# Four attention layers as one stream of units, with norms, projections and output stages woven between them

## The chip, the cores and the metric

One core of a Trainium2 chip. The time is the device time of one execution in microseconds (us); medians are over several executions. The granted TensorE clock is given as a share of full speed.

## The reference

The input is 2048 tokens of 640 features in bf16. Two kinds of layer alternate, A, B, A, B: A attends causally within a window of 256 tokens, B attends to all tokens. Each has 32 heads of 20 features.

```python
x = x + A(layernorm(x), A_wqkv, A_wo)
x = x + B(layernorm(x), B_wqkv, B_wo)
x = x + A(layernorm(x), A_wqkv, A_wo)      # the same weights again
x = x + B(layernorm(x), B_wqkv, B_wo)

def layer(x, wqkv, wo):                    # A and B; cut
    q, k, v = split_heads(x @ wqkv)        # 32 heads of 20
    scores = q @ k.T * 20 ** -0.5
    # A only: keep 0 <= query - key < 256, others to -1e9
    return softmax(scores) @ v @ wo
```

B needs the keys and values of all 2048 tokens before any unit of it can end. A needs only the tokens up to its own.

## The kernel before

A *unit* is four heads (group `g` of 8) by 512 queries (chunk `c` of 4): 32 units per layer. The four heads lie in four bands of 32 partitions. A *bank* is the scores of one head, 128 keys by 512 queries, one PSUM bank. A full unit has 64 banks, a windowed one 12. Three banks make a *tile*: TensorE computes its scores, ScalarE (ACT in the profile) takes the exponential of all three at once, VectorE (DVE) multiplies it with a 0/1 mask in the windowed layers, and two tiles later TensorE multiplies it with V into the unit's one output bank `op`. The rows' sums come from a column of ones in V.

The layers run one after another, each as norm, then projections, then attention, and output stages as units end:

```python
psS = tc.tile_pool(name="psS", bufs=2, space=PSUM)   # scores, 2 x 3 banks
psO = tc.tile_pool(name="psO", bufs=1, space=PSUM)   # op, 1 bank
psM = tc.tile_pool(name="psM", bufs=1, space=PSUM)   # everything else, 1 bank
...
for lidx in range(4):
    ...  # norm of all 16 token blocks, transposed into xnT
    ...  # K of all groups, V of all blocks
    for t in range(len(tiles) + PV_LAG):
        ...
        for u in tiles[t]: project_q(u + 1)            # Q of the next unit, once
        sp = psS.tile(...)                             # scores of tile t
        nc.scalar.activation(out=pt, in_=sp, func=Exp, scale=SCALE)
        if windowed: nc.vector.tensor_tensor(out=pt, in0=pt, in1=mask, op=mult)
        ...                                            # V of tile t - 2 into op
        if end: finish_unit(u)
        run_due()
```

When a unit ends, `finish_unit` copies `op` to SBUF on VectorE (`oT`); only then may the next unit write `op`. Its *tail* follows in small steps that go to and fro between TensorE and VectorE: row sums (`zp`), reciprocals split in two bf16 parts (`hl`), a transpose (`rp`), a copy (`rT`), a spread over the partitions (`zb`), the product (`on`). After eight units of a chunk comes the output projection (`yp`), added to `x_sb`.

The softmax here doesn't subtract the row's maximum and nothing guards it: scores larger than these inputs give would overflow.

Of the kernel before, what the change touches and what calls it, by code (L numbers as in the profile page):

```python
# [7 lines left out]
BF16 = mybir.dt.bfloat16  # L8
# [11 lines left out]
G = 8  # L20
# [4 lines left out]
HD = D // 2  # L25
PV_LAG = 2


@with_exitstack
def kernel(  # L30
# [11 lines left out]
    ctx.enter_context(nc.allow_low_precision("bf16 operands of the matmuls"))  # L42

    const = ctx.enter_context(tc.tile_pool(name="const", bufs=1))
    big = ctx.enter_context(tc.tile_pool(name="big", bufs=1))

    xin = A_x.flatten_outer_dims().rearrange("(t p) d -> p t d", p=P)
    xout = out.flatten_outer_dims().rearrange("(t p) d -> p t d", p=P)

    x_sb = big.tile([P, NT, D], BF16, name="x_sb", tag="x_sb")  # L50
    for c in range(NC):
        nc.sync.dma_start(out=x_sb[:, 4 * c : 4 * c + 4, :], in_=xin[:, 4 * c : 4 * c + 4, :])

    wpads = []
    for which in range(2):
        wq = big.tile([P, KD, G, P], BF16, name=f"wq{which}", tag=f"wq{which}")
        wk = big.tile([P, KD, G, P], BF16, name=f"wk{which}", tag=f"wk{which}")
        wpads.append((wq, wk))
    with tc.tile_pool(name="stg", bufs=2) as stg:
        for which, wqkv in ((0, A_wqkv), (1, B_wqkv)):  # L60
            wq, wk = wpads[which]
            st = stg.tile([P, KD, 2 * D], BF16, name="st", tag="st")
            nc.scalar.dma_start(
                out=st[:], in_=wqkv.rearrange("(c p) f -> p c f", p=P)[:, :, 0 : 2 * D]
            )
            for w, off in ((wq, 0), (wk, D)):
                nc.gpsimd.memset(w[:], 0.0)
                for dc in range(KD):
                    dst = w[:, dc, :, :].rearrange("p g (j m) -> p (g j) m", j=4)[:, :, 0:DH]
                    src = st[:, dc, off : off + D].rearrange("p (h e) -> p h e", h=H)  # L70
                    nc.vector.tensor_copy(out=dst, in_=src)  # L71

    wpool = ctx.enter_context(tc.tile_pool(name="wts", bufs=1))
    lnp = ctx.enter_context(tc.tile_pool(name="lnp", bufs=2))
    xnp = ctx.enter_context(tc.tile_pool(name="xnp", bufs=2))
    qp = ctx.enter_context(tc.tile_pool(name="qp", bufs=3))
    ptp = ctx.enter_context(tc.tile_pool(name="ptp", bufs=4))
    otp = ctx.enter_context(tc.tile_pool(name="otp", bufs=2))
    onp = ctx.enter_context(tc.tile_pool(name="onp", bufs=1))
    rzp = ctx.enter_context(tc.tile_pool(name="rzp", bufs=2))  # L80
    psS = ctx.enter_context(tc.tile_pool(name="psS", bufs=2, space=bass.MemoryType.PSUM))
    psO = ctx.enter_context(tc.tile_pool(name="psO", bufs=1, space=bass.MemoryType.PSUM))
    psM = ctx.enter_context(tc.tile_pool(name="psM", bufs=1, space=bass.MemoryType.PSUM))

    xnT = big.tile([P, KD, S], BF16, name="xnT", tag="xnT")
    kT = big.tile([P, G, S], BF16, name="kT", tag="kT")
    v_all = big.tile([P, NT, H, 32], BF16, name="v_all", tag="v_all")
    nc.gpsimd.memset(v_all[:], 0.0)
    nc.gpsimd.memset(v_all[:, :, :, DH : DH + 1], 1.0)

    nhalf = const.tile([P, 4], F32, name="nhalf", tag="nhalf")
    nc.gpsimd.memset(nhalf[:], -0.5)
    ident = const.tile([P, P], BF16, name="ident", tag="ident")
# [5 lines left out]
    sel4 = const.tile([P, 4], BF16, name="sel4", tag="sel4")  # L99
    nc.vector.tensor_copy(  # L100
        out=sel4[:], in_=ident[:].rearrange("p (j m) -> p j m", j=4)[:, :, DH]
    )

    spread4 = const.tile([32, 4, P], BF16, name="spread4", tag="spread4")
    sp32 = const.tile([32, 2, 16], BF16, name="sp32", tag="sp32")
    nc.vector.tensor_copy(
        out=sp32[:], in_=ident[0:32, 0:32].rearrange("p (n r) -> p n r", n=2)
    )
    sp16 = const.tile([32, 16], BF16, name="sp16", tag="sp16")
    nc.vector.tensor_tensor(out=sp16[:], in0=sp32[:, 0, :], in1=sp32[:, 1, :], op=ALU.add)  # L110
    nc.vector.tensor_copy(
        out=spread4[:].rearrange("p q (j m) -> p (q j) m", m=32),
        in_=sp16[:].unsqueeze(2).to_broadcast((32, 16, 32)),
    )

    masks = const.tile([P, 3, C], BF16, name="masks", tag="masks")
    nc.gpsimd.memset(masks[:], 1.0)

    def mask_block(m, b, ge):
        v = masks[:, m, b * P : (b + 1) * P]  # L120
        if ge:
            nc.gpsimd.affine_select(
                out=v, in_=v, compare_op=ALU.is_ge, fill=0.0,
                base=0, pattern=[[1, P]], channel_multiplier=-1,
            )
        else:
            nc.gpsimd.affine_select(
                out=v, in_=v, compare_op=ALU.is_gt, fill=0.0,
                base=0, pattern=[[-1, P]], channel_multiplier=1,
            )  # L130


    for m, b, ge in (
        (0, 0, False), (0, 1, True), (0, 3, False),
        (1, 1, False), (1, 2, True),
        (2, 0, True), (2, 2, False), (2, 3, True),
    ):
        mask_block(m, b, ge)
# [16 lines left out]
    deferred = []  # L155
    clock = [0]

    def later(n, fn):
        deferred.append((clock[0] + n, fn))

    def run_due(everything=False):
        while deferred and (everything or deferred[0][0] <= clock[0]):
            deferred.pop(0)[1]()

    for lidx in range(4):
        which = lidx % 2
        windowed = which == 0
        wqkv, wo = (A_wqkv, A_wo) if windowed else (B_wqkv, B_wo)
        wq, wk = wpads[which]
        wv = wpool.tile([P, KD, D], BF16, name="wv", tag="wv")  # L170
        nc.sync.dma_start(
            out=wv[:], in_=wqkv.rearrange("(c p) f -> p c f", p=P)[:, :, 2 * D : 3 * D]
        )
        wop = wpool.tile([P, G, D], BF16, name="wop", tag="wop")
        nc.gpsimd.memset(wop[:], 0.0)  # L175
        wo_v = wo.rearrange("(g j e) f -> j e g f", g=G, j=4)
        for j in range(4):
            nc.sync.dma_start(out=wop[32 * j : 32 * j + DH, :, :], in_=wo_v[j])

        with tc.manual_schedule():  # L180

            for c in range(NC):
                mv = lnp.tile([P, 4, 2], F32, name="mv", tag="mv")
                for i in range(4):
                    tb = 4 * c + i
                    stats = lnp.tile([P, 2, 6], F32, name="stats", tag="stats")
                    nc.vector.bn_stats(out=stats[:, 0, :], in_=x_sb[:, tb, 0:HD])
                    nc.vector.bn_stats(out=stats[:, 1, :], in_=x_sb[:, tb, HD:D])
                    nc.vector.bn_aggr(out=mv[:, i, :], in_=stats[:])
# [253 lines left out]
```

## Time and profile before

| | before |
|---|---|
| median of 4 runs beside the changed kernel | 3253.48 us (3252.39 to 3254.67) |
| TensorE busy, mean clock in the stages | 77%, 0.60 to 1.00 |
| ScalarE busy | 70% |
| VectorE busy | 26% |
| HBM traffic | 15 MB, 5 GB/s |

The page, the windows by stage and two timelines are shown in the prediction. Two lines of the list of waits are added here. Each line names the instruction that waited, what released it, the sum in us, the number of waits and the longest.

```profile
PE op L396 <- DVE oT L275: 187.6, 114, 2.7
...
PE pq L258 <- DVE rT L300: 103.1, 58, 2.8
```

### The profile page before, as it was taken

Reading aid. Unit: us, or ns where it says so; the run is one execution under the profiler, and the core shown is the slowest. Engines: PE = TensorE matmul, PEld = TensorE weight load, DVE = VectorE, ACT = ScalarE, POOL = GpSimd, SP = SyncE. Lnnn points to the kernel's source line nnn. Section 1 sums busy time; section 2 is a strip of 40 time slices with the busy share of each in tenths; the row PEclk is TensorE's granted clock in tenths of the full one; section 3 lists DMA queues with packets and bytes.
Section 4 is the critical chain, followed back from the end, with each engine's and each line's share of the span. In section 5 each row is a group of like instructions: output and inputs, shape, how many; then the busy total and the mean of one; then the engine's idle time right before and its main releaser. Section 6 shows DMA issues by size and latency. Waiting matters only on the chain.

```text
span 3250.1 us, 36154 instructions
## 1 busy us (share of the span) xinstructions
PE 2509.4 (77%) x15292; PEld 882.9 (27%) x15424; DVE 836.5 (26%) x1800; ACT 2286.0 (70%) x1815; POOL 74.9 (2%) x58
## 2 busy tenths in 40 slices
PE   1866566988888888888886665678888888888887
PEld 1422223422222222222243222243222222222222
DVE  6355556210100111010045555541111001011101
ACT  1334344499799989979934334337997997997996
POOL 5000000000000000000000000000000000000000
PEclk9966666856655565565587665686656556566555
DMA  2000000000000000000000000000000000000000
GB/s 93 11 1 1 1 1 11 11 1 1 1 1 1 1 1 1 1 1 1 1 11 11 1 1 1 1 11 1 1 1 9 1 1 9 1 1 9 1 1 9
DMA packets 11042, 17.38 MB, mean 5 GB/s; under 512 B 384, under 2 KB 9600, under 8 KB 10880
## 3 DMA queue, kind: packets, MB, share of 16 engines
q1 hardware_dynamic: 9568, 11.80, 1.3%
q10 hardware_dynamic: 1312, 3.28, 0.3%
q8 instruction: 120, 1.97, 0.3%
q14 instruction: 42, 0.34, 0.0%
HBM read 12.45 MB, written 2.62 MB: 5 GB/s over the span
## 4 chain that ended last, share of the span: by engine, by line
ACT 40%; PE 29%; issue 16%; DVE 13%; POOL 1%; DMA 0%; ACTq 0%; POOLq 0%; DVEq 0%
ACT pt L367 40%; PE pq L258 8%; DVE pt L382 5%; PE yp L323 5%; PE sp L354 5%; PE pk L224 4%; PE op L396 3%; PE pv L239 3%; DVE x_sb L329 2%; DVE oT L275 2%; DVE on L309 1%; DVE wq L71 1%; POOL wop L175 1%; PE trp L211 1%; POOL rstd L195 0%
## 5 line engine op out<-in xcount | busy, mean ns | idle before, releaser
L367 ACT ACTIVATE pt<-sp 128x1536 bf16<-128x1536 f32 (+2 forms) x1654 | 2183.7, 1504 | 623.0 <-PE sp L354 617.6
L354 PE MATMUL sp<-qt,kT 32*128 32x512 bf16 (+3 forms) x5504 | 938.9, 509 | 245.5 <-ACT pt L367 243.7
L396 PE MATMUL op<-pt,v_all 128*32 128x512 bf16 (+3 forms) x5504 | 948.6, 523 | 189.6 <-DVE oT L275 187.6
L354 PEld LDWEIGHTS <-kT 32*128 32x128 bf16 x5504 | 300.6, 99 | 834.0 <-issue 824.5
L263 DVE CAST qt<-pq 128x512 bf16<-128x512 f32 x128 | 88.6, 692 | 1465.6 <-PE pq L258 1465.6
L396 PEld LDWEIGHTS <-v_all 128*32 128x32 bf16 x5504 | 188.0, 101 | 807.4 <-issue 807.2
L258 PE MATMUL pq<-xnT,wq 128*128 128x512 bf16 x524 | 253.8, 593 | 130.1 <-DVE rT L300 103.1
L382 DVE TENSOR_TENSOR pt<-pt,masks 128x1536 bf16<-128x1536 bf16 (+4 forms) x384 | 240.1, 654 | 153.0 <-ACT pt L367 152.7
L323 PE MATMUL yp<-wop,on 128*128 128x320 bf16 x1024 | 188.7, 335 | 63.4 <-DVE x_sb L329 60.1
L323 PEld LDWEIGHTS <-on 128*128 128x128 bf16 x1024 | 109.0, 108 | 140.5 <-issue 91.5
L224 PE MATMUL pk<-xnT,wk 128*128 128x512 bf16 x624 | 142.9, 388 | 2.3 <-issue 0.9
L258 PEld LDWEIGHTS <-wq 128*128 128x128 bf16 x640 | 76.9, 129 | 245.1 <-issue 237.6
L215 ACT COPY xnT<-trp 128x640 bf16<-128x640 bf16 x64 | 41.4, 694 | 137.9 <-PE trp L211 137.9
L275 DVE CAST oT<-op 128x512 bf16<-128x512 f32 x128 | 88.0, 687 | 176.9 <-PE op L396 176.8
L231 ACT CAST kT<-pk 128x1024 bf16<-128x1024 f32 x32 | 32.4, 1012 | 114.1 <-PE pk L224 114.1
L309 DVE TENSOR_TENSOR on<-oT,zb 128x512 bf16<-128x512 bf16 x128 | 87.5, 684 | 92.8 <-PE zb L305 92.7
L211 PE MATMUL trp<-ident,xn 128*128 128x128 bf16 x320 | 36.2, 280 | 88.5 <-DVE xn L204 85.9
L329 DVE TENSOR_TENSOR x_sb<-x_sb,yp 128x320 bf16<-128x320 bf16 x128 | 62.2, 486 | 159.5 <-PE yp L323 159.4
L239 PE MATMUL pv<-wv,xnT 128*128 128x320 bf16 x640 | 87.6, 299 | 0.0
L224 PEld LDWEIGHTS <-wk 128*128 128x128 bf16 x640 | 64.2, 100 | 80.3 <-issue 8.9
L305 PE MATMUL zb<-rT,spread 32*128 32x128 bf16 x512 | 70.9, 283 | 4.1 <-DVE rT L300 3.9
L239 PEld LDWEIGHTS <-xnT 128*128 128x128 bf16 x640 | 62.6, 98 | 24.9
(42 smaller groups left out, 589.4 us busy)
## 6 DMA issues: line engine op xcount, KB each, us to landing
x_sb<-in_A_x_dram SPq DMA_DIRECT2D x4, 640.0 KB
out_dram<-x_sb SPq DMA_DIRECT2D x4, 640.0 KB
st<-in_A_wqkv_dram ACTq DMA_DIRECT2D x1, 1600.0 KB
st<-in_B_wqkv_dram ACTq DMA_DIRECT2D x1, 1600.0 KB
wv<-in_A_wqkv_dram SPq DMA_DIRECT2D x2, 800.0 KB
wop<-in_A_wo_dram SPq DMA_DIRECT2D x8, 200.0 KB
wv<-in_B_wqkv_dram SPq DMA_DIRECT2D x2, 800.0 KB
wop<-in_B_wo_dram SPq DMA_DIRECT2D x8, 200.0 KB
```

The lines of the kernel that those rows point to most:

```text
L224: nc.tensor.matmul(pk[:, i, :], lhsT=wk[:, dc, g, :], rhs=xnT[:, dc, (c0 + i) * C : (c0 + i + 1) * C], start=(dc == 0), stop=(dc == KD - 1),)
L239: nc.tensor.matmul(pv[:, i, 0:HD], lhsT=xnT[:, dc, tb * P : (tb + 1) * P], rhs=wv[:, dc, i * HD : (i + 1) * HD], start=(dc == 0), stop=(dc ...
L258: nc.tensor.matmul(pq[:], lhsT=wq[:, dc, g, :], rhs=xnT[:, dc, c * C : (c + 1) * C], start=(dc == 0), stop=(dc == KD - 1),)
L263: nc.vector.tensor_copy(out=qt[:], in_=pq[:])
L275: nc.vector.tensor_copy(out=oT[:], in_=ops.pop(u)[:])
L309: nc.vector.tensor_tensor(out=on[:, g, :], in0=oT[:], in1=zb[:], op=ALU.mult)
L323: nc.tensor.matmul(yp[:], lhsT=on[:, g, qb * P : (qb + 1) * P], rhs=wop[:, g, i * HD : (i + 1) * HD], start=(g == 0), stop=(g == G - 1),)
L329: nc.vector.tensor_tensor(out=xv, in0=xv, in1=yp[:], op=ALU.add)
L354: nc.tensor.matmul(sp[:, i, col * P : (col + qn) * P], lhsT=kT[32 * j : 32 * j + 32, g, kc * P : (kc + 1) * P], rhs=qts[u][32 * j : 32 * j ...
L367: nc.scalar.activation(out=pt[:, i:n, b0 * P :], in_=sp[:, i:n, b0 * P :], func=ACT.Exp, scale=SCALE,)
L382: nc.vector.tensor_tensor(out=pt[:, i:n, b0 * P :], in0=pt[:, i:n, b0 * P :], in1=mv_, op=ALU.mult,)
L396: nc.tensor.matmul(ops[u][32 * j : 32 * j + 32, q0 * P : (q0 + qn) * P], lhsT=v_all[:, kc, 4 * g + j, :], rhs=pt[:, i, col * P : (col + qn ...
```

## The change

Its intent: give ScalarE exponentials from the start to the end, by putting all other work of TensorE between the tiles of one stream that crosses the layers.

- One list of units for all layers. Layer 1's later chunks are interleaved with layer 2's windowed units (and layer 3's first chunk with the last of them).
- Norms, projections, tails and output stages become generators. After the scores of each tile, `pump` lets them emit a few TensorE instructions, against a credit in us (0.73 for three banks, 0.30 for two). Where a unit needs something not yet made, `require` emits it all at once: a *lump*.
- Score tiles alternate between three and two banks, so that `psM` gets two buffers.
- K, Q and V of the full layers go to HBM and come back, one unit ahead.
- The padded weights for Q and K are made per group, written to HBM once and read back from then on.
- The values carry 21 columns per head instead of 32.

The core of the diff, with many cuts:

```diff
-    psS = ctx.enter_context(tc.tile_pool(name="psS", bufs=2, space=bass.MemoryType.PSUM))
-    psM = ctx.enter_context(tc.tile_pool(name="psM", bufs=1, space=bass.MemoryType.PSUM))
+    psS = pool("psS", 1, PS)          # tags sa (3 banks) and sb (2 banks)
+    psM = pool("psM", 2, PS)
 ...
+    units = [Unit(0, c, g) for c in range(NC) for g in range(G)]
+    units += [Unit(1, 0, g) for g in range(G)]
+    for c in range(1, NC + 1):
+        small = deque(Unit(2, c - 1, g) for g in range(G))
+        for g in range(G if c < NC else SPLIT):
+            units.append(Unit(1, c, g) if c < NC else Unit(3, 0, g, "a"))
+            if g >= 1:
+                for _ in range(2):
+                    if small:
+                        units.append(small.popleft())
+        units += small
 ...
+    def load_unit(u):
+        nc.sync.dma_start(out=vt[key]..., in_=v_d[l]...)
+        nc.sync.dma_start(out=kt[key]..., in_=k_d[l]...)
+        nc.sync.dma_start(out=qt[key]..., in_=q_d[l]...)
 ...
+    def t_tail(l, c, g, on, oT):
+        yield ("wait", 2)
+        ...                            # zp, rz, hl
+        yield ("wait", 1)
+        ...                            # rp, rT
+        yield ("wait", 1)
+        ...                            # zb, on
 ...
-            tiles = [banks[i : i + 3] for i in range(0, len(banks), 3)]
+            size = 3 if len(tiles) % 2 == 0 else 2
+            tiles.append(banks[n : n + size])
 ...
+            pump(0.43 * n_b + 0.06 - 0.62 if n_b else 2.0)
+            while pts and pts[0][0] <= t - PV_LAG:
+                ...                    # V of an earlier tile into op
```

## The prediction

> **What bounds the kernel now.** I read the page first, for the shares and the 40 slices.
>
> ```profile
> PE 2509.4 (77%) x15292; PEld 882.9 (27%) x15424; DVE 836.5 (26%) x1800; ACT 2286.0 (70%) x1815; POOL 74.9 (2%) x58
> ...
> ACT  1334344499799989979934334337997997997996
> ...
> PEclk9966666856655565565587665686656556566555
> ...
> L367 ACT ACTIVATE pt<-sp 128x1536 bf16<-128x1536 f32 (+2 forms) x1654 | 2183.7, 1504 | 623.0 <-PE sp L354 617.6
> L354 PE MATMUL sp<-qt,kT 32*128 32x512 bf16 (+3 forms) x5504 | 938.9, 509 | 245.5 <-ACT pt L367 243.7
> L396 PE MATMUL op<-pt,v_all 128*32 128x512 bf16 (+3 forms) x5504 | 948.6, 523 | 189.6 <-DVE oT L275 187.6
> ```
>
> ACT works 2286 us of 3250, nearly all of it exponentials, but in two different regimes: 9 tenths in the full layers, 3 to 4 tenths elsewhere. TensorE looks busier on average, at a granted clock near 0.6. Next, busy time by stage: start, windowed layer 0, the dense prologue of layer 1, its full attention.
>
> ```profile
> 0.00:138.00 138.00, 70.21 (x415) 41.00 (x421) 72.25 (x118) 27.50 (x42) 47.43 (x31) 1.00 0.19 61
> 138.00:557.00 419.00, 259.47 (x2125) 108.92 (x2151) 231.29 (x502) 177.47 (x156) 3.60 (x6) 0.65 0.00 1
> 557.00:630.00 73.00, 63.48 (x357) 34.90 (x359) 23.35 (x39) 19.26 (x31) 5.57 (x3) 0.93 0.10 23
> 630.00:1656.00 1026.00, 865.88 (x4801) 261.19 (x4829) 123.26 (x305) 925.60 (x692) 3.60 (x6) 0.60 0.00 1
> ```
>
> Columns after the length: PE, weight loads, DVE, ACT, POOL, clock. Layers 2 and 3 repeat this. ACT bounds the full stages (926 of 1026 us, 32 us per unit of 64 banks). The windowed stages have no full engine: ACT 42%, DVE 55%, PE 62%, so a serial chain sets them. The dense prologues leave ACT idle. The timeline shows both regimes:
>
> ```profile
> 938.08 0.61 PE L396 MATMUL op<-pt,v_all 128*32 128x512 bf16 x3
> ...
> 938.88 0.61 PE L354 MATMUL sp<-qt,kT 32*128 32x512 bf16 x3 [0.19 <-ACT pt L367]
> ...
> 939.42 0.61 PE L396 MATMUL op<-pt,v_all 128*32 128x512 bf16 x3
> ...
> 942.44 0.40 PE L396 MATMUL op<-pt,v_all 128*32 128x512 bf16 x3
> ...
> 942.62 28.54 ACT L367 ACTIVATE pt<-sp 128x1536 bf16<-128x1536 f32 x21 [1.10 <-PE sp L354]
> ```
> ```profile
> 282.94 1.45 ACT L367 ACTIVATE pt<-sp 128x1536 bf16<-128x1536 f32 x1 [1.80 <-PE sp L354]
> ...
> 285.56 0.58 PE L258 MATMUL pq<-xnT,wq 128*128 128x512 bf16 x1 [2.02 <-DVE rT L300]
> ```
>
> In the full layer a tile of three banks comes every 1.35 us on ACT (28.54 less the 0.19 tail, over 21). PE waits 0.19 us for it each time; sp to op is 0.54 us at half clock (938.88 to 939.42). At 942 ACT lost 1.10 us to the query projection of the next unit. In the windowed layer the projection waits for a DVE copy because psM has one buffer, and the next exponential waits for the projection: 11.66 us per unit whose exponentials take 5.3. Last, the clock in short windows:
>
> ```profile
> 936.00:940.00 4.00, 3.44 (x21) 0.89 (x20) 0.00 (x0) 4.00 (x5) 0.00 (x0) 0.50 0.00 0
> ...
> 942.00:944.00 2.00, 1.49 (x13) 0.48 (x13) 0.69 (x1) 1.38 (x2) 0.00 (x0) 1.00 0.00 0
> ...
> 946.00:950.00 4.00, 4.00 (x32) 1.26 (x30) 0.82 (x4) 3.88 (x4) 0.00 (x0) 0.50 0.00 0
> ```
>
> It is 0.50 or 1.00 and nothing between. Attention alone leaves it at 0.50, even with PE 100% busy (946 to 950); a full-array projection of some 2 us lifts it for one stretch of about 3.4 us.
>
> **What the Trainium skill says.** "TensorE: Matmul & The Clock Gate", Part 1: the PE clock has two states, half and full, chosen by busy-ness in a free-running window of about 3.4 us. The trace agrees in values and window length; that attention matmuls in a quarter of the array do not count as enough is this trace's own finding. "ScalarE: Activation LUTs", "What ACT_TABLE_LOAD costs": an ACTIVATE with immediate operands takes 186 ns plus 0.833 ns per column, neighbours overlapping by about 93. That makes 1.37 us per 1536 columns; the trace has 1.35. "TensorEngine Tiling (Array Packing)", "Key Properties": a change of tiling mode drains the array. The trace agrees: 512 columns at half clock are 0.43 us, but the step is 0.54. "Perfetto Trace Analysis", "Optimization Strategy" advises interleaving regimes with different limits, which is this change.
>
> **The change part by part.** The matmul count on PE is identical in the two programs (both streams have 30850 rows). What changes is order and packing.
>
> 1. *Score tiles.* Five banks are split 3+2 instead of 3+3, freeing one for a second psM buffer. 1946 tiles replace 1622. Two banks cost ACT 1.35 - 0.43 = 0.92 us, so a pair costs 2.26, 1.13 per tile on average. Exponentials rise from 2184 to about 1946 x 1.13 = 2200 (less some 15 for the short first chunks): +1%. For PE it is worse: two banks need the same 0.54 + 0.54 us as three, so attention alone costs PE 2.16 us of each 2.26 at half clock, but 1.30 at full clock (0.65 per tile: 942.12, 942.44, 942.76 are its steps).
> 2. *Weaving.* About 620 us of full-clock PE work (1280 projection matmuls at 0.216, 1664 of 320 columns at 0.136, transposes, the sums of units) is put in tile by tile, up to about 0.96 us per pair. Counting the program's PE order: tiles with heavy fill cluster in 39 bursts that cover 756 of 1946 tiles. In a burst at full clock PE needs 1.30 + 0.96 = 2.26 of 2.26: just balanced.
> 3. *Evacuations* stay on ACT until layer 1's first full unit (about 77 us), then go to DVE.
> 4. *K, Q, V through HBM.* Each full unit reads about 1 MB, one unit ahead, in 29 us: 34 GB/s where this chip's start moved 390. Hidden.
> 5. *Start.* The weight pads are built per group instead of 24 + 5 us of copies before the first norm; the first exponential comes at about 25 us (4 arrival, 5 statistics, 3 norm, 4 transposes, 6 values, 3 q and k) instead of 138.
>
> Time, stage by stage (the fill of each tile counted from the program):
>
> - Start: **25**.
> - Layer 0 inside the stream, 154 tiles. PE 154 x 0.65 + 76 fill = 176; ACT 165 + 28 evacuations = 193; DVE about 49 per chunk for masks and unit sums plus 20 for weight pads = 215. Three near-equal engines and masks between ACT and PE: I take **245**.
> - Work forced out in lumps where a chunk needs it: the program has 9.7, 18.4, 23.7 and 41.1 us in single tiles. 93 of PE, with evacuation gaps **100**.
> - Layer 1, first chunk, 205 tiles: ACT 232, PE 243 in the filled part: **246**.
> - Layers 1, 2 and the start of 3, 921 tiles: ACT 921 x 1.13 = 1041. Losses: about 20 bursts that begin at half clock, 2.5 us each until the clock rises = 50; about 20 isolated pairs of projections (2.2 us at full, 4.3 at half clock), 2.5 each = 50; one lump 12; windowed units whose masks and sums need more DVE (6.3) than ACT (5.4), 32 x 1. **1185**.
> - The rest of layer 3, 666 tiles, half clock, PE 96% plus 1.3 us of sums per unit: 753 + 25 = **778**.
> - End (28 now): **21**.
>
> Sum 25 + 245 + 100 + 246 + 1185 + 778 + 21 = **2600 us**. Of the 654 gained, the two windowed layers and the prologues give about 500, since layer 2's 490 us shrink to the exponentials that it adds to the stream; taking full units from 32 to about 29.5 us gives about 150.
>
> **The rivals.** (a) *The clock stays at half in the bursts.* PE would then need 1946 x 1.08 + 2 x 620 = 3340 us: no gain. For it: 946 to 950, busy and still 0.50. Against: the dense prologues run at 0.93 to 1.00 and one projection suffices to lift the clock. About 3%. (b) *ACT as the clean bound:* everything hides, 2200 + 77 + 46 = 2325, perhaps 2420 with the lumps. For it: ACT ran 21 tiles unbroken in the full layer. Against: PE is at 96 to 100% of ACT's pace both with and without fill, so there is no slack to absorb a wait. (c) *DVE's order:* one op bank must be emptied by DVE, behind masks and copies; PE stands still meanwhile. If windowed units still took 9 us, 64 of them would add some 100: about 2700. (d) *HBM round trips* exposed at unit starts, 64 x 3 us at most: 2750; the loads are one unit ahead, so unlikely.
>
> **Range and chances.** 2600, with 80% in 2440 to 2770: below by (b), above by (c), (d) or slower clock rises. Faster by over 2%: 0.96; within 2%: 0.02; slower: 0.02.
>
> **What would show it.** First exponential near 25 us; ACT about 2280 busy us and 85 to 90% of the span; clock 1.00 in bursts and 0.50 in the last 750 us; ACT idle named after PE; gaps in the exponentials before chunks 1 to 3 of layer 0 and at layer 1's start; no waits on DMA. I am wrong if bursts run at 0.50, if ACT waits for DVE through masks, or if a large share of idle falls on loads.

## The result, and the profile after

The changed kernel is correct and takes 2925.94 us (median of 4 runs, 2923.31 to 2931.94), against 3253.48 for the kernel before on the same chip. The ratio is 0.8996, with a 95% interval of 0.8979 to 0.9012. Ratios here and below are the mean time of one kernel's runs over that of the other's of the same rounds, so not quite the ratio of the medians quoted. The direction was right, but 2926 lies well outside the predicted 2440 to 2770.

The first sections of the page of the changed kernel, to be set against the ones in the prediction:

```profile
PE 2551.2 (87%) x15325; PEld 837.1 (29%) x15424; DVE 876.4 (30%) x1959; ACT 2309.9 (79%) x2099; POOL 46.8 (2%) x113
...
ACT  4554561788978789878887888777599999999997
...
PEclk8777878998585599756986579866856556556555
```

ScalarE does the work that was expected (2310 us; about 2280 predicted), but at 79% of the span, not 85 to 90%. The row of slices shows three stretches: 4 to 5 tenths in the first six slices (layer 0), 7 to 9 in the middle, 9 at the end. The windows of the four stages, from the first exponential to the last, with columns as in the prediction:

```profile
27.80:522.00 494.20, 364.05 (x2669) 159.18 (x2700) 264.68 (x622) 237.30 (x281) 19.96 (x46) 0.77 0.13 40
522.00:783.00 261.00, 242.20 (x1368) 73.26 (x1383) 57.41 (x104) 234.84 (x202) 0.00 (x0) 0.83 0.16 54
783.00:2132.00 1349.00, 1162.65 (x7386) 395.97 (x7433) 463.82 (x1012) 1067.01 (x938) 14.56 (x40) 0.75 0.18 52
2132.00:2912.00 780.00, 758.13 (x3757) 193.59 (x3756) 69.55 (x181) 762.25 (x666) 0.00 (x0) 0.55 0.11 35
```

In layer 0 no engine is near full: TensorE 74% (99 of its 15424 matmuls are missing from this trace), VectorE 54%, ScalarE 48%. In the last stage ScalarE is at 98%. So the loss lies before the last stage, where windowed units are in the stream and where the lumps are. Set against the sum of the prediction, with the tiles counted in the trace (the measured row of layer 0 runs up to the fourth lump, which stands three tiles into layer 1; some 4 us of its 88 belong to the row of layer 1):

| step | predicted, us | measured, us | miss |
|---|---|---|---|
| start, to the first exponential | 25 | 27.8 | +3 |
| layer 0 inside the stream (154 tiles) | 245 | 332.6 | +88 |
| lumps (gaps of 23.7, 40.8, 29.3, 67.6) | 100 | 161.4 | +61 |
| layer 1, first chunk | 246 | 261.5 | +16 |
| the 921 tiles after it | 1185 | 1348.6 | +164 |
| the rest of layer 3 (666 tiles) | 778 | 780.1 | +2 |
| end | 21 | 18.2 | -3 |
| sum | 2600 | 2930.2 | +330 |

The waits that answer to the two lines of before:

```profile
ACT pt L771 <- PE sb L758: 216.6, 103, 67.6
...
ACT pt L771 <- PE sa L758: 160.7, 137, 6.2
...
PE op L799 <- DVE oT L641: 77.3, 87, 2.9
...
PE zb L682 <- DVE rT L677: 55.6, 33, 5.5
...
PE rp L675 <- DVE hl L671: 31.1, 21, 4.4
```

ScalarE waits for TensorE (99 of the 216.6 us are two lumps, of 67.6 and 31.5), and TensorE in its turn for small VectorE results: the copy of `op` and two steps of the tail. One place in the middle of the stream shows how, in the timeline (start, length, engine, line, operation, and in brackets the idle time before it and what ended it):

```profile
1689.86 1.61 DVE L786 TENSOR_TENSOR pt<-pt,masks 128x1536 bf16<-128x1536 bf16 x2 [0.92 <-ACT pt L771]
...
1691.38 0.68 DVE L641 CAST oT<-op 128x512 bf16<-128x512 f32 x1
...
1692.12 0.62 PE L799 MATMUL op<-pt,va 128*21 128x128 bf16 x8 [1.63 <-DVE oT L641]
...
1693.33 1.02 ACT L771 ACTIVATE pt<-sb 128x1024 bf16<-128x1024 f32 x1 [1.25 <-PE sb L758]
...
1695.91 1.03 DVE L786 TENSOR_TENSOR pt<-pt,masks 128x512 bf16<-128x512 bf16 x2 [0.83 <-ACT pt L771]
...
1697.35 0.17 DVE L671 TENSOR_TENSOR hl<-rz,hl 128x16 bf16<-128x16 f32 x1
...
1697.57 0.29 PE L675 MATMUL rp<-ident,hl 128*32 128x128 bf16 x1 [1.93 <-DVE hl L671]
...
1698.84 1.45 ACT L771 ACTIVATE pt<-sa 128x1536 bf16<-128x1536 f32 x1 [2.05 <-issue]
```

Read it from the top. VectorE is on a mask when the last product of a unit lands in `op`, so the copy of `op` starts only at 1691.38. TensorE's next instruction is the first product of the next unit; it needs `op` and stands for 1.63 us. The scores of the next tile are behind it in TensorE's order, so ScalarE loses 1.25 us. Four us later the same happens through the tail: the mask of 1695.91 had waited 0.83 us for its exponential, and the reciprocals queued behind it; TensorE waits 1.93 us for `hl`, and ScalarE then loses 2.05 us (the profile calls it "issue", but the scores that it needed had just come). VectorE is only 34% busy in this stage (463.8 of 1349), and 59% among these windowed units (11.85 us of 1690 to 1710). So it is not full here; what TensorE waits for stands in its order.

The other loss is the lumps. The largest, between layers 0 and 1, as a window and in the timeline:

```profile
454.30:521.80 67.50, 49.52 (x318) 30.72 (x318) 38.76 (x94) 0.00 (x0) 4.89 (x10) 0.85 0.23 67
```
```profile
487.64 0.45 PE L324 MATMUL trp<-ident,xn 128*128 128x128 bf16 x5 [1.14 <-DVE xn L316]
488.13 0.49 DVE L236 COPY xnT<-trp 128x640 bf16<-128x640 bf16 x1 [0.55 <-PE trp L324]
488.54 0.44 DVE L316 TENSOR_SCALAR xn<-x_sb,rstd,nmr 128x640 bf16<-128x640 bf16 x1
...
492.59 5.16 PE L354 MATMUL pv<-wv,xnT 128*128 128x320 bf16 x20
...
520.62 0.61 PE L799 MATMUL op<-pt,vt 128*21 128x512 bf16 x4 [6.30 <-DMA vt<-v_d]
```

TensorE has 41 us of full-clock work here and takes 67.5: 18 us idle, and the rest at a mean clock of 0.85. The norm is a serial chain of some 1.4 us per 128 tokens (scale on VectorE 0.44, five transposes 0.45, copy 0.49, with hand-overs), TensorE idling 1 us of each. After it the projection of 20 matmuls ran at half clock (5.16 us). At the end the values of the first unit had to come back from HBM, 6.30 us.

### The profile page after: what moved, and what is told of

The parts are those of the page before. It is cut to its first block, busy times and chain, and to the rows that moved or that the text cites. A ratio compares the mean times of both kernels' runs of the same rounds, so it can differ in the third digit from the quotient of the medians.

```text
span 2930.2 us, 37851 instructions
## 1 busy us (share of the span) xinstructions
PE 2551.2 (87%) x15325; PEld 837.1 (29%) x15424; DVE 876.4 (30%) x1959; ACT 2309.9 (79%) x2099; POOL 46.8 (2%) x113
## 5 line engine op out<-in xcount | busy, mean ns | idle before, releaser
L771 ACT ACTIVATE pt<-sa 128x1536 bf16<-128x1536 f32 (+3 forms) x993 | 1416.6, 1429 | 203.3 <-PE sa L758 160.7
L771 ACT ACTIVATE pt<-sb 128x1024 bf16<-128x1024 f32 (+2 forms) x983 | 1004.2, 1023 | 256.1 <-PE sb L758 216.6
L799 PE MATMUL op<-pt,vt 128*21 128x512 bf16 x4096 | 853.5, 514 | 34.6 <-DVE oT L641 15.6
L758 PE MATMUL sa<-qt,kt 32*128 32x512 bf16 x2458 | 433.3, 512 | 60.7 <-ACT pt L771 40.6
L758 PE MATMUL sb<-qt,kt 32*128 32x512 bf16 x1638 | 426.9, 514 | 15.4 <-ACT pt L771 10.3
L786 DVE TENSOR_TENSOR pt<-pt,masks 128x1024 bf16<-128x1024 bf16 (+5 forms) x422 | 247.4, 610 | 514.6 <-ACT pt L771 513.5
L275 PE MATMUL pq<-xnT,wqk 128*128 128x512 bf16 x1181 | 371.7, 446 | 33.8 <-DMA wqk<-wqk_d 16.6
L758 PEld LDWEIGHTS <-kt 32*128 32x128 bf16 x4096 | 211.4, 96 | 642.3 <-issue 624.1
L799 PEld LDWEIGHTS <-vt 128*21 128x21 bf16 x4096 | 164.1, 92 | 584.7 <-issue 564.3
L799 PE MATMUL op<-pt,va 128*21 128x384 bf16 (+2 forms) x1408 | 153.3, 348 | 71.7 <-DVE oT L641 61.8
L682 PE MATMUL zb<-rT,spread 32*128 32x128 bf16 x512 | 67.7, 272 | 56.5 <-DVE rT L677 55.6
L686 DVE TENSOR_TENSOR on<-oT,zb 128x512 bf16<-128x512 bf16 x128 | 87.7, 685 | 78.4 <-PE zb L682 78.2
```

The source lines that it names most:

```text
L275: nc.tensor.matmul(pq[:], lhsT=wt[:, n, dc, :], rhs=xt[:, dc, :], start=(dc == 0), stop=(dc == KD - 1),)
L682: nc.tensor.matmul(zb[:, qb * P : (qb + 1) * P], lhsT=spread4[:, qb, :], rhs=rT[:], start=True, stop=True,)
L686: nc.vector.tensor_tensor(out=on[:, g, :], in0=oT[:], in1=zb[:], op=ALU.mult)
L758: nc.tensor.matmul(sp[:, i, col * P : (col + qn) * P], lhsT=u.k(kc, j), rhs=u.q(j, q0, qn), start=True, stop=True,)
L771: nc.scalar.activation(out=pt[:, i:k, b0 * P :], in_=sp[:, i:k, b0 * P :], func=ACT.Exp, scale=SCALE,)
L786: nc.vector.tensor_tensor(out=pt[:, i:k, b0 * P :], in0=pt[:, i:k, b0 * P :], in1=mv_, op=ALU.mult,)
```

## The experiments

Every kernel but one starts from the changed kernel or a combination of its variants; all ran with 3 timed rounds or more. "Stage times" are the stages of the table above, from each trace. For orientation, the theories:

- **T1, order**: TensorE, in order, stands for small VectorE results that are queued behind masks, which themselves wait for exponentials. This is rival (c) of the prediction.
- **T2, dependency**: masks lie between the exponential and the product with V, two tiles is too short for them.
- **T3, lumps** and work that comes too late.
- **T4, loads** from HBM (rival (d)).
- **T5, packing**: alternating three and two banks costs TensorE more than it frees.

The expectations have numbers of their own: their Theory 1 is T1, their Theory 3 is T3 with T4, and their Theory 2 is another one, that TensorE has too much to do in the windowed stretches at half clock.

### Leaving the masks out (wrong result)

```diff
-                    if m is not None:
+                    if False:
```

> Wrong result on purpose: the mask multiplications of the windowed units are left out, nothing else. In the changed kernel ACT stands idle about 158 us in layer 0 and 143 us in layer 2 before exponentials that lie within three tiles of a windowed unit. Theory 1 (the in-order TensorE waits for small VectorE results that queue behind masks, which themselves wait for exponentials): two thirds of this goes, about 2725 us. Theory 2 (windowed stretches are slow because TensorE has too much to do there, at half clock): the TensorE work is unchanged, so at most 40 us go, 2885 or more. Theory 3 (lumps and HBM round trips): no change, 2910 to 2925.

Measured: 2734.92 us, ratio 0.8409 (0.8395 to 0.8424): 191 us less than the changed kernel. Layer 0 inside the stream went from 332.6 to 241.1 us, against the 245 of the prediction, and the 921 tiles from 1348.6 to 1256.3. Lumps and the last stage did not move. Of the waits:

```profile
PE op L799 <- DVE oT L641: 32.4, 81, 0.9
```

77.3 had become 32.4, with as many waits (81 for 87) and none above 0.9 us, about the length of the copy alone. The waits for `rT` and `hl` fell from 86.7 to 15.8. So masks account for 191 of the miss of 326. The Theory 2 of the expectation falls: it allowed 40 us, since the TensorE work is unchanged. Whether the masks cost by T1 or T2 this run does not tell.

### Masks kept in VectorE's queue, but nobody waits for them (wrong result)

```diff
+    scr = big.tile([P, 3, C], BF16, name="scr", tag="scr")
...
-                            out=pt[:, i:k, b0 * P :], in0=pt[:, i:k, b0 * P :], in1=mv_,
+                            out=scr[:, i:k, b0 * P :], in0=pt[:, i:k, b0 * P :], in1=mv_,
```

> Wrong result on purpose: the mask multiplications run as before on VectorE, reading the same exponentials, but write to a scratch tile, so the value matmuls no longer wait for them. It separates two parts of what leaving out the masks gave (190 us). If TensorE waited for the masks themselves: most of it is gained, about 2770. If it waited for copies and unit sums that queue behind the masks in VectorE: nearly nothing, 2890 to 2925.

Measured: 2939.38 us, ratio 0.9035 (0.9022 to 0.9049), no gain, even 13 us longer. The products with V no longer depended on the masks, and the waits for `oT`, `rT` and `hl` stayed at 78.9, 55.6 and 33.2 us. T2 falls. What costs is that masks sit in VectorE's queue ahead of small results.

### More tiles between the steps of the tail

```diff
-        yield ("wait", 1)        # before rp, and again before zb
+        yield ("wait", 3)
```

> Correct result. The two later steps of a unit's sums (the transpose rp and the spread zb) are issued three tiles after the step before instead of one, so that VectorE has its operand ready when TensorE gets there. Theory 1: the TensorE waits named zb after DVE rT and rp after DVE hl (55.6 and 31.1 us in the changed kernel) go, 40 to 60 us less, about 2875. Theories 2 and 3: no change.

Measured: 2845.65 us, ratio 0.8744 (0.8729 to 0.8759), 80 us less, more than the 40 to 60 expected. The waits of `rp` for `hl` and of `zb` for `rT` are all but gone (0.8 and 0.3 us in sum). That for `oT` grew from 77.3 to 100.3, so part of the time went over to the next wait in line. Layer 0 inside the stream fell by 34 us, the 921 tiles by 45. T1, shown with a correct kernel and two numbers changed.

### The products with V one tile later

```diff
-PV_LAG = 2
+PV_LAG = 3
-    ptp = pool("ptp", 4)
+    ptp = pool("ptp", 5)
```

> Correct result. The value matmuls follow the scores by three tiles instead of two (and the probability tiles have five buffers instead of four), so masks have one tile more before TensorE needs them. Theory 1: if the wait is for the mask itself, 60 us or more go, about 2860; if it is for the copies that queue behind masks, little. Theory 2 and 3: no change.

Measured: 2907.29 us, ratio 0.8933 (0.8918 to 0.8948), 19 us less. Layer 0 inside the stream did not change (335.8). A small gain, as expected if TensorE does not wait for the masks themselves. The waits for `oT`, `hl` and `rT` changed places (73.7, 78.4 and 10.9 us, from 77.3, 31.1 and 55.6), but their sum stayed, 163 us for 164. Where the 19 us come from was not found.

### The copy of `op` of windowed units on ScalarE

```diff
-            nc.vector.tensor_copy(out=oT[:], in_=op[:])
+            (nc.scalar.copy if u.windowed else nc.vector.tensor_copy)(out=oT[:], in_=op[:])
```

> Correct result. The copy that empties the single output bank of a windowed unit runs on ACT instead of VectorE, so it no longer queues behind masks; ACT gets 64 copies of about 0.58 us, 37 us more. Theory 1, with the output bank as the main wait (TensorE waits 61.8 us for DVE oT before windowed value matmuls): the gain outweighs the cost, 2870 to 2900. Theory 2: 37 us slower, 2960.

Measured: 2902.98 us, ratio 0.8925 (0.8912 to 0.8938), 23 us less, although 64 copies were added to the busiest engine of the later stages. The waits for `op` fell to 58.7 us, those of the tail stayed (34.5 for `hl`, 56.7 for `rT`).

### The last three together

Edit: the three above.

> Correct result. Three edits together: the sums of a unit spaced by three tiles (alone 80 us), values three tiles behind (alone 19), output bank emptied by ACT in windowed units (alone 23). If they remove different waits of the same chain they add up: 2925 - 122 = about 2803. If the same wait moves from one to the next: 2830 to 2845.

Measured: 2827.07 us, ratio 0.8692 (0.8679 to 0.8705), 99 us less; the three gains alone add up to 122.

```profile
PE op L799 <- ACT oT L641: 31.4, 39, 1.5
...
PE op L799 <- DVE oT L641: 22.9, 26, 2.2
```

Waits for `op` are down to 54 us in all, and those of the tail for `hl` to 2.8. ScalarE's idle time before windowed tiles without woven work, summed over the 921 tiles of the trace, fell from 64.3 to 8.9 us; before windowed tiles *with* woven work only from 79.0 to 70.7. (Windowed: within three tiles after a windowed bank. With woven work: a projection, a norm's transposes or an output projection stands in TensorE's order between the scores two tiles before and the scores one tile after. The split moves with the second definition; the sums, 143 and 80 us, do not.) About half as much as the masks cost can thus be had back by order alone, with a correct result. Against the run without masks 56 us remain in layer 0 and 33 in the 921 tiles; there the idle time before windowed tiles with woven work stands at 70.7 us against 52.

### Fewer mask columns

```diff
+                        lo, hi = (max(b0, 1) * P, 3 * P) if m == 1 else (b0 * P, C)
-                            out=pt[:, i:k, b0 * P :], ...
+                            out=pt[:, i:k, lo:hi], ...
```

One of the three masks is all ones in its outer two blocks of 128 columns; they need no multiply.

> Correct result. A dose of the same suspect: in one of the three kinds of masked banks only the two middle blocks are multiplied (the other two are all ones), which takes about a sixth of the mask time out of VectorE's queue. Leaving out all masks gave 190 us. Theory 1 (what queues behind masks): 20 to 45 us, about 2895. If only the complete absence of a mask behind an exponential helps (each mask still waits for its exponential, and the small steps behind it wait too): under 15 us.

Measured (5 rounds): 2912.3 us, ratio 0.8959 (0.8934 to 0.8984), 14 us less, with overlapping intervals. VectorE's mask work fell from 247 to 218 us. Taking away 12% of the work gave 7% of what taking away all of it gave. That is under the 20 to 45 us that the expectation drew from T1. But 12% of 191 would be 23 us, and the intervals leave room for anything from nothing to 25: whether the cost goes with the amount of mask work, this run cannot tell.

### Half of the masks on GpSimd

```diff
-                        nc.vector.tensor_tensor(
+                        (nc.vector if t % 2 == 0 else nc.gpsimd).tensor_tensor(
```

> Correct result. The masks of every other tile (those of two banks) are multiplied on GpSimd instead of VectorE. Theory 1 in its sharper form after the scratch-tile run (small VectorE results queue behind masks that wait for exponentials): about 40% of the mask time leaves that queue, 40 to 80 us less, about 2865, if GpSimd multiplies 1024 columns in under 2 us; if it takes longer, the value matmuls wait for it and the gain is gone, 2930 to 3000.

Measured: 2978.74 us, ratio 0.915 (0.9136 to 0.9164), 53 us *longer*. One might think that the product with V now waits for the slow masks, but TensorE's waits on them come to 4.0 us. Its waits for `oT` rose from 77.3 to 116.3. The groups by shape of GpSimd and VectorE (count, sum, mean ns) and a place in the timeline tell why:

```profile
L786 POOL TENSOR_TENSOR pt<-pt,masks 128x1024 bf16<-128x1024 bf16 x95 | 206.1, 2170 | 564.4 <-ACT pt L771 562.8
```
```profile
L786 DVE TENSOR_TENSOR pt<-pt,masks 128x1024 bf16<-128x1024 bf16 x63 | 65.2, 1035 | 197.3 <-ACT pt L771 197.3
```
```profile
1689.85 2.12 POOL L786 TENSOR_TENSOR pt<-pt,masks 128x1024 bf16<-128x1024 bf16 x1 [4.71 <-ACT pt L771]
1690.12 1.87 DVE L670 CAST hl<-rz 128x16 bf16<-128x16 f32 x1
```

A mask of 1024 columns takes 2.17 us on GpSimd, and the masks that stayed on VectorE take 1035 ns where they took 689. A copy of 16 columns, 0.17 us elsewhere, takes 1.87 us and ends with GpSimd's mask. VectorE is held up while GpSimd works, so the small results that TensorE waits for came later, not sooner. (GpSimd itself is hardly held up: its shortest mask of this shape took 2113 ns, the mean is 2170.) The edit did not take the masks out of VectorE's way.

### A larger credit in layer 0

```diff
-            pump(0.43 * n_b + 0.06 - 0.62 if n_b else 2.0)
+            pump(0.43 * n_b + 0.06 - (0.32 if cur and cur[0][0].l == 0 else 0.62) if n_b else 2.0)
```

> Correct result. While layer 0's units are emitted, the budget of other work per tile is raised by 0.3 us, so that less of it is left to be forced out in a lump before the next chunk. In the changed kernel the five lumps take 24, 41, 29, 68 and 32 us of ACT idle time, 193 us for 104 us of full-clock TensorE work. If lumps lose time because nothing else runs beside them, moving work out of the first four saves 40 us or more, about 2880. If layer 0 is bound by the amount of TensorE and VectorE work, the work only moves: 2910 to 2940.

Measured: 2868.47 us, ratio 0.8817 (0.8802 to 0.8833), 57 us less, but **the result was wrong, which was not intended**. The cause was not tested; I infer that the weights of B were loaded over those of A in their shared buffer before the last padded weights of A had been made from it, since the greater credit reorders the two, and the data flow within this manual schedule follows the order of the program. The combinations below, with the same credit and a guarded order, are correct, which fits. The time is still that of the same work in another order: the lump at tile 38 vanished and the other three of layer 0 and the start of layer 1 fell from 137.7 to 96.3 us, while the stream between them took 9 us more. This is T3.

### Weight pads of layer 1 earlier and apart, in a guarded order

```diff
+        while ("qk", 0, 0, G - 1) not in ready:      # A's pads first
+            yield ("wait", 1)
         nc.sync.dma_start(out=raw[:], in_=wq_view[1][:, :, 0 : 2 * D])
-        yield ("wait", 8)
+        yield ("wait", 6)
         for g in range(G):
             get_w(1, g, True)
-            yield ("pe", 0.5)
+            yield ("wait", 3)
```

(Also cut: no use of B's pads before they are all written, and this task is queued ahead of the next chunk's.)

> Correct result. The eight weight pads for layer 1 are made one every three tiles during layer 0's first chunk instead of all inside the second lump, where VectorE waited for their stores and TensorE 7.5 us for VectorE. If the lumps are long because of such things put in them, 10 to 20 us less: about 2910. If the lump is bound by other steps: 2920 to 2926.

Measured: 2920.11 us, ratio 0.8976 (0.8958 to 0.8993), 6 us less, with overlapping intervals. In the trace the second lump shrank from 40.8 to 28.6 us: in the changed kernel TensorE had stood there 7.48 us for `x_sb`, whose addition queued in VectorE behind copies of weight pads, each of which waited for the store of an earlier one. The gain of 12 us in the lump is shown, its arrival in the total is not.

### Windowed units spread singly

```diff
-                for _ in range(2):
+                for _ in range({2: 1, 3: 1, 4: 1, 5: 1, 7: 0}.get(g, 2) if c < NC else 2):
```

> Correct result. In the mixed stretches most windowed units of layer 2 stand alone between two full units instead of in pairs. Theory 1 (a queue of masks and small steps on VectorE): VectorE has a full unit's 29 us to catch up after each, so the 143 us of idle time around windowed units of layer 2 fall by a quarter, about 2890. If each windowed unit pays by itself, no change: 2915 to 2930.

Measured: 3003.39 us, ratio 0.9226 (0.9209 to 0.9244), 77 us *longer*. ScalarE's idle time before windowed tiles hardly moved (64.3 to 54.9 without woven work, 79.0 to 83.8 with it), where a quarter less was expected: a windowed unit pays by itself, alone or in a pair. And layer 2 now ended too late for what depends on it: the lumps in the 921 tiles grew from one of 31.5 us to five of 136.9 in all. T3 again, from the other side: the order of the units had been chosen to keep work off the deadline.

### Projections broken off when the credit is spent

```diff
         if state["held"] is not None:
-            return state["held"]
+            return None if blocked else state["held"]
```

> Correct result. A projection or output group may be broken off when the tile's budget is spent and goes on in the next tile, instead of being issued whole (1.08 us at full clock behind one score tile). In the changed kernel ACT stands idle 25 + 100 us in front of exponentials with such work and no windowed unit near. If the whole groups are the cause: 50 to 80 us less, about 2860. If the cause is that TensorE is at half clock or full there: no change, 2910 to 2930.

Measured: 2995.3 us, ratio 0.9201 (0.9185 to 0.9217), 69 us *longer* by the medians. In the two traces, whose executions differ by 54, all stages with woven work grew: 22 us in layer 0 inside the stream, 17 each in layer 1's first chunk and in the 921 tiles. Five matmuls in one go cost less than the same five apart. More switches between attention and dense matmuls, or bursts too thin to lift the clock, would both do that; they were not told apart.

### Each load from HBM done twice

```diff
+        for _ in range(2):
             nc.sync.dma_start(out=vt[key]..., in_=v_d[l]...)      # the same for kt and qt
```

> Correct result. Every load of K, Q and V from HBM is done twice into the same tile, which doubles the suspect of rival (d) of the prediction and of the lumps (round trips through HBM). If the loads are hidden, as the prediction took them to be: within 15 us of the changed kernel, 2920 to 2940. If round trips at unit starts cost what rival (d) allowed, some 3 us at each of 64 unit starts, doubling adds 60 us or more: 2980.

Measured: 3017.2 us, ratio 0.9281 (0.9263 to 0.9299), 91 us *longer*. The second load of a pair waits for the first, in the queue of SyncE, through which all transfers go:

```profile
SPq L563 <- DMA vt<-v_d: 213.7, 70, 7.1
SPq L572 <- DMA kt<-k_d: 209.7, 62, 5.3
```

That is 3.1 and 3.4 us each. TensorE's waits for the arrival of weights, V, Q and K rose from 53 to 130 us. So the loads were not free of charge in principle: there was little slack, and hardly for want of bandwidth (the changed kernel moves 52 GB/s in the stage of the 921 tiles, where the start of the kernel before reached 390); they stand in one queue. It does not yet tell what single loads cost; that is left for the last run.

### The kernel before with the new packing alone

```diff
-    psS = ctx.enter_context(tc.tile_pool(name="psS", bufs=2, space=bass.MemoryType.PSUM))
+    psS = ctx.enter_context(tc.tile_pool(name="psS", bufs=1, space=bass.MemoryType.PSUM))
-    psM = ctx.enter_context(tc.tile_pool(name="psM", bufs=1, space=bass.MemoryType.PSUM))
+    psM = ctx.enter_context(tc.tile_pool(name="psM", bufs=2, space=bass.MemoryType.PSUM))
-            tiles = [banks[i : i + 3] for i in range(0, len(banks), 3)]
+            ...                        # three and two banks in turn
```

> One part of the change alone, in the kernel before: score tiles of three and two banks in turn, the freed bank as a second psM buffer; layers one after the other as before. The prediction's step 1: full layers at half clock have TensorE at 96% of ACT's pace, so the query projections and unit sums cost about 1 us more per unit (64 us), while the windowed layers lose the wait of the projection for psM (103 us). Sum near zero: 3200 to 3260. If the packing itself were most of the gain of the change, 3000 or less.

Measured: 3254.07 us, ratio 1.0006 (0.9991 to 1.0021): nothing. The windows of layers 0 and 1, as in the prediction, show why:

```profile
138.00:557.00 419.00, 297.36 (x2191) 114.16 (x2189) 244.43 (x534) 182.91 (x184) 9.17 (x9) 0.62 0.01 3
...
630.00:1656.00 1026.00, 952.89 (x4755) 263.56 (x4752) 122.52 (x293) 920.54 (x812) 6.76 (x5) 0.62 0.00 1
```

TensorE needs 953 us in the full stage where it needed 866. From the first exponential of a stage to the last, a windowed stage became 17 us shorter (the second `psM` buffer), a full one 20 us longer (0.62 us per unit). T5 is true in part and comes out at zero; the packing by itself gives none of the gain. Not all of the rest is weaving: the first exponential comes at 27.8 us instead of 137.0, which is 109 of the 327 us gained, since only the first chunk's share of pads, norm and projections stands before it.

### Combinations

The three edits of the tail, the lag and `oT`, with the guarded weight pads and the larger credit of layer 0:

> Correct result. The three edits of the earlier combination (2827), weight pads spread (alone 6) and the larger budget in layer 0 (alone 57, there with a wrong result from the order of the weight pads, which is mended here). If the lumps' loss and the queue's loss are independent: 2827 - 6 - 57 = 2764. If moving work out of lumps into windowed tiles feeds the same VectorE queue: 2790 to 2815.

Measured: 2778.97 us, ratio 0.8542 (0.853 to 0.8555), correct. Within layer 0 there is one lump left of 28.4 us in place of three of 94; the one at layer 1's start takes 56.2 for 67.6. The time lies between the two expected, 2764 and 2790 to 2815: the stream inside layer 0 took 28 us more than with the three edits alone.

The same with seven instead of six units of layer 3's first chunk begun early (`SPLIT = 7`):

> Correct result. The one before, with seven instead of six units of layer 3 begun on the first twelve key blocks, so that the last chunk's norm, values and projections have another 22 us of attention beside them. The lump of 32 us at the start of the second parts should fall by about 20 us, the rest unchanged: 20 us under the one before. If the lump only moves, no change.

Measured: 2775.71 us, ratio 0.8536 (0.8522 to 0.855): the same, within the intervals. The lump of 34.3 us before the last stage fell to 15.9 while the last stage grew from 777.3 to 787.1.

The same with fewer mask columns, which had given 14 us alone:

> Correct result. The one before, with the shortened masks too. Theory 1: 10 to 30 us under it. If the earlier edits have already removed all that waits behind masks: no change.

Measured: 2758.18 us, ratio 0.848 (0.8466 to 0.8494), 18 us less, now with intervals apart: a small gain, but a real one.

And, last, the same with the reads of K, Q and V issued from GpSimd's queue instead of SyncE's:

```diff
-        nc.sync.dma_start(out=vt[key]..., in_=v_d[l]...)
+        nc.gpsimd.dma_start(out=vt[key]..., in_=v_d[l]...)      # the same for kt and qt
```

> The best combination so far (2758 us), with one difference: the reads of K, Q and V for the full units are issued from GpSimd's queue, while the reads and writes of the weight pads and the writes of K, Q and V stay in SyncE's. Theory that the loads had no slack because all of them stand in one queue, each issued only after the one before has found its buffer or its data: TensorE's waits on the arrival of V, K, Q and of the weight pads (about 14 us for V alone in the combination's trace) shrink, and the time falls to 2725-2750. Rival (d) of the prediction in its 'nil' form, that at single loads the queue never holds up anything: 2753-2763. Third, that issuing costs more from GpSimd, which also builds the pads of V and the reciprocal roots of the norms, so that waits on POOL appear: 2765-2800.

Measured: 2744.56 us (2742.65 to 2748.24), ratio 0.8442 (0.8428 to 0.8456), 14 us less than the run before, and correct: the best of all, 6.2% under the changed kernel (0.8442 over 0.8996) and 15.6% under the kernel before. In the run before, writes of Q and K to HBM had stood ahead of the reads in SyncE's queue, each waiting for VectorE's copy:

```profile
SPq L409 <- DVE st L236: 148.2, 57, 6.9
...
SPq L435 <- DVE kt L236: 106.7, 8, 19.3
```

Reads that TensorE then waited for had been issued just after such a write (at 457.2, 527.4, 554.5 and 1928.8 us); in the new trace these waits are gone, and only those at the start of layer 1 and before the last stage are left, where the data had just been written. TensorE's waits for the arrival of K, Q and V fell from 32 to 17 us, by about as much as the time. The "nil" form of rival (d) falls here; single loads cost something like 15 us through the shared queue, and no more than the 32 that were waited for. What this costs in the changed kernel itself (36 us of such waits) was not run.

## Why the prediction was right or wrong

**Right.** The order of events was as told: first exponential at 27.8 us for 25; ScalarE 2310 us for 2280; half clock with TensorE at 97% in the last stage (0.55 in the mean of the stage), 780 us for 778; a clock near 1 in woven stretches; lumps before chunks 1 to 3 of layer 0, at layer 1's start and once later, where the program had them. The main bet, that weaving makes the dense work fit beside ScalarE, held: the losses given to bursts and isolated projections, 50 + 50 us over the 921 tiles, measure 100 us of ScalarE's idle time before full tiles with woven work. Only the sum is measured; that both halves are right is not shown, and it may be luck in part. Rival (a) is dead, rival (b) would have needed what no version reached.

**Wrong, first: "I take 245" for layer 0, and "32 x 1" for windowed units.** The stages with windowed units were taken as three engines with nearly equal sums of work, plus a little. Sums do not hold where one engine's order stands in another's. Layer 0 took 333 us. Without masks it took 241, so the 245 is what the sum is worth when no mask stands in VectorE's queue, and the missing 88 us are masks. In the 921 tiles ScalarE's idle time before windowed tiles was 143 us (64.3 and 79.0), for which 32 were set; leaving the masks out took 92 us off this stage. The mechanism had been named, as rival (c): "one op bank must be emptied by DVE, behind masks and copies; PE stands still meanwhile". But it was put beside the sum, not in it, and at some 100 us. The runs show 191, and none of it through the masks' own dependency (no gain with that cut). For about half of it they show that order alone is the cause (80 us from two numbers in the tail's spacing, 99 us from three edits). Whether the other half is order too, or the amount of mask work, they leave open (12% less of it: 14 us, hardly clear of noise). The prediction's own sign of being wrong, "if ACT waits for DVE through masks", came true at one remove: ScalarE waits for TensorE, and TensorE for what is queued behind masks. The prediction looked for such waits only at `op`; the tail's `hl` and `rT` cost as much, 87 us of TensorE's waits beside 77.

**Wrong, second: "100" for the lumps.** TensorE's work in them was counted well (93 us; the trace has 95, half-clock time counted half), but they measured 161: TensorE stood idle for 49 us of it and lost 18 to the half clock. To take a lump at TensorE's rate needs work that keeps it fed. These contain norms, a chain of small steps on three engines; in the largest, two of the value projections after a norm ran at half clock (0.54 in 492.6 to 497.6, 0.50 in 508.8 to 514.3); one includes a round trip through HBM. A later lump took 31.5 us for 12. Together 80 us of the miss. The larger credit with the guarded pads removed some of it: the stretch from the first exponential to the end of the lump at layer 1's start came from 494 us down to 403 in the combination with fewer mask columns (319 inside the stream, 27 and 57 in two lumps), still 58 above the 245 + 100 of the prediction.

**Wrong in part: "Hidden" for K, Q and V.** Bandwidth was the wrong measure (34 against 390 GB/s). The loads are hidden most of the time, but each waits in one queue behind others that wait for their data or their buffers; where no waits on DMA were expected, TensorE had 53 us of them. Shown is a cost of 14 us, in the best kernel.

**The sum of the miss.** 191 us by the masks' removal; about 58 in the lumps before layer 1 and 19 in the later one, both still there without masks; the remaining 60 or so are spread over layer 1's first chunk and the windowed and woven tiles.

**What stays open.** Without masks the 921 tiles still take 71 us more than predicted (19 of them the later lump), and 52 us of ScalarE's idle time lie before windowed tiles with woven work. Bursts that are "just balanced" leave nothing to absorb a wait, which would explain it, but no run isolates it. A slip of the prediction points the same way: it gives a burst 0.96 us of other work per pair of tiles, which is what fits (2.26 less 1.30), while the program's credit is 1.03. Over the 378 pairs of its bursts that is some 26 us, as an estimate from these numbers. Of the 191 us, about half was recovered with a correct kernel.

## What to carry to other kernels

When two regimes are woven into one stream, add up the engines' work, then ask for each in-order engine which small result of another it stands for, and what may stand ahead of that result in its queue: here a reciprocal of 0.25 us behind a mask behind an exponential held up TensorE and then ScalarE. Spacing such a hand-over by two more tiles was worth 2.7% of the time. Count forced work by its chain, not by its engine's sum, and give deadlines slack before giving the stream balance: the two experiments that disturbed the order of units or of matmul groups lost 69 and 77 us.

## What the Trainium skill lacked or had wrong

- "Perfetto Trace Analysis", "Optimization Strategy" advises interleaving regimes with different limits. It helped (0.8996), but the section does not say that the in-order queues of both regimes are then coupled: 191 us went with the masks of one regime, of which none was due to the masks' own dependency (13 us longer without it).
- "TensorE: Matmul & The Clock Gate", Part 1 has the clock follow busy-ness. Attention matmuls in a quarter of the array leave it at 0.50 although TensorE is 100% busy (the window of 946 to 950 us of the kernel before), and so in the last stage of the changed kernel: 758 of 780 us busy, clock 0.55. The part does not say what keeps such matmuls from counting as busy. Whether it is the quarter of the array, or that a step takes 0.54 us where 512 columns take 0.43, no run here separates.
- "GPSIMD Engine Reference", 4.1 Engine selection puts GpSimd at about twice VectorE's time for two-input elementwise work. Here a bf16 mask of 1024 columns took 2170 ns on GpSimd in the mean, and never under 2113, with VectorE at work beside it, against 689 on VectorE alone: 3.1 times. Its section "8. Key points" says that GpSimd shares its SBUF interfaces with VectorE, and the trace agrees: beside it VectorE's masks of the same shape went from 689 to 1035 ns, a copy of 16 columns from 0.17 to 1.87 us.
- "Trainium Kernel Development and Optimization", Key Constraints says that issuing transfers from several engines only saves the sequencer's issue time. Moving the reads of K, Q and V from SyncE's queue to GpSimd's also kept them from standing behind writes that waited for their data: TensorE's waits for them fell from 32 to 17 us and the time from 2758 to 2745.
- No page that was read gives a price for a chain of small steps across engines. The norm's took 1.4 us per 128 tokens for 0.44 + 0.45 + 0.49 us of work with one step in flight, and TensorE idled 1 us of each.
